# A gated unit in plain float32, in pairs of half-width matmuls, in place of three products of split parts

## The chip, the cores and the metric

The kernel runs on one core of a Trainium2 chip. The metric is the device time of one execution in microseconds. TensorE is called PE in the profile, VectorE DVE, ScalarE ACT, GpSimd POOL and SyncE SP; `PEld` is the load of a stationary operand into TensorE. Line numbers such as L699 are those of the kernel before.

## What is computed

The input is `x` of 2048 tokens by 448 features. It is normalised over the features, and two branches work on the result; their sum and `x` itself are the output.

```python
xn = _layernorm(x, axis=-1)
return x + _A_ref(xn, ...) + _B_ref(xn, B_w_gate, B_w_up, B_w_down)

# _A_ref: a long convolution along the tokens, one kernel of 2048 taps per feature
K = 2.0 * jnp.einsum("dn,dnl->dl", C, P).real      # P = exp(A dt * position), 256 states
y = irfft(rfft(u, 4096) * rfft(K, 4096))[:2048] + u * D_skip

# _B_ref: the gated unit, 1792 hidden features
g = jnp.einsum("bsd,df->bsf", x, w_gate)
u = jnp.einsum("bsd,df->bsf", x, w_up)
return jnp.einsum("bsf,fd->bsd", _sigmoid(g) * u, w_down)
```

All inputs and outputs are float32.

## The kernel before

Two generators, `conv()` and `glu()`, yield small steps, each with a weight that stands for its length, and a loop at the end always advances the generator that has done the smaller share of its total. So the two branches are spread over each other evenly, and the instruction order on each engine follows from that; `hp(HP)` gives an instruction a high priority, `tc.issue_after(x)` keeps one behind another. The totals stand in a list, where 14.8 is the planned length of one hidden tile of the gated unit:

```python
total = [sum(Y0) + 11 * WP + 8 * WX + 14 + NCK * WK + HOLE + 17 * WS, 2 * (4 + NFT * 14.8) - HELD]
```

`conv()` has three stages.

- A first stage loads and normalises x, transposes it for the gated unit (`x_transpose`), and prepares the parameters of the convolution kernels (`prep`, on DVE and ACT), with a first transform of x (`x_spec`).
- The generator `kgen` makes the convolution kernels in 56 steps of 8 features. In each step, POOL makes tables of magnitudes (`magnitudes`, L495 and L507), TensorE makes phases (`tr`, L529), ACT takes their sines (L537 to L540), DVE multiplies both (`Et` and `Ft`, L591 to L593), and TensorE sums over the states (`ko`, L607, four tiles of 32 columns side by side). Every four steps two banks of small 64x64 products follow (`kp` and `kq`, L555).
- `spectra` goes over frequencies in 17 steps. `there` transforms kernels and x (`sp`, L892), DVE multiplies them, `back` transforms to the time domain (`pv`, L919), a copy goes through memory (`v_d`, `vp`), and `last` makes the last transform (`pv`, L954) and adds it to the accumulators.

All these products but `tr` are of plain float32. In `there`, the output is made in halves of 64 partitions: for each of two feature halves `j` and each of two sources, the two real and imaginary parts `c` and two frequencies `i` make four matmuls, where `i` selects the half of the output partitions. At the single frequency step (`k == 32`, the `sx,t` and `skl,t` groups of the profile) there is one `i`, so all of its matmuls go to one half.

`glu()` takes the tokens in two halves of 1024, each as two blocks `t` of 512, and the hidden features in 14 tiles of 128, in groups of three or two (`FCH`). For each hidden tile and each `t` there is one gate: `gate` makes g and u in two PSUM banks named `gu` (four in all, shared with the down products `po`), ACT takes a tanh (`th`), and DVE makes `hf` from both. After each group the down products add it, for eight blocks of 128 tokens, to accumulators in SBUF (`acc`, L815).

TensorE takes float32r operands here, which have fewer bits than float32. So each operand is split into a high part and the rest: x into `xh` and `xl` (with the last 64 of the 448 features packed as high and low in `xr`), the weights into `wh` and `wl`, the hidden activations into `hh` and `hl` (L715, L717), the down weights into `dh` and `dl` (L779, L780). A product is then three: high by high, low by high, high by low. For one gate these are 11 matmuls of 128x128 by 512 columns for g and 11 for u (L699); one block of a down product takes three matmuls of 448 columns per hidden tile (L810). The weights of nine hidden tiles are split once and both parts stored to memory (`wt_d`, `dt_d`), to be loaded again for the second half of the tokens; those of the other five (`RAW`) are loaded and split a second time, on POOL.

Of the kernel before, what the change touches and what calls it, by code (L numbers as in the profile page):

```python
# [15 lines left out]
ALU = mybir.AluOpType  # L16
# [14 lines left out]
WS = 4.5  # L31
# [4 lines left out]
HELD = 9  # L36
# [4 lines left out]
RB = 2  # L41
# [4 lines left out]
RAW = set(GROUPS[0] + GROUPS[1][1:])  # L46
# [82 lines left out]
def s4d_glu_kernel(ctx, tc, io):  # L129
# [14 lines left out]
    wt_d = dram.tile([2, NFT, 128, 8 * 128], F32, name="wt_d")  # L144

    v_d = dram.tile([2, 128, 32, H], F32, name="v_d")
    dt_d = dram.tile([2, NFT, 128, D], F32, name="dt_d")
# [43 lines left out]
    def x_transpose(src, xs, o0):  # L191

        xh, xl, xr = xs
# [6 lines left out]
        for k in range(4):  # L200
            kp = 128 if k < 3 else 64
            at = k * nb % 4
            if nb == 4:
                ps = banks[k]
            elif at == 0:
                ps = psg.tile([128, 512], F32, name="gu", bufs=4)
            for b in range(nb):
                c = 128 * (at + b)
                nc.tensor.transpose(ps[:kp, c : c + 128], src[b][:, 128 * k : 128 * k + kp], ident)
            p = ps[:kp, 128 * at : 128 * (at + nb)]  # L210
            if k == 0 and nb == 2:
                continue
            if k == 1 and nb == 2:
                p = ps.rearrange("p (k t) -> p k t", k=2)
                nc.scalar.copy(xh[:, 0:2, o], p)
                v.tensor_tensor(xl[:, 0:2, o], p, xh[:, 0:2, o], ALU.subtract)
            elif k < 3:
                nc.scalar.copy(xh[:, k, o], p)  # L218
                v.tensor_tensor(xl[:, k, o], p, xh[:, k, o], ALU.subtract)
            else:  # L220
                mv = nc.scalar.copy(xr[0:64, o], p)
                xls[:] = [v.tensor_tensor(xr[64:128, o], p, xr[0:64, o], ALU.subtract)]
                act[:] = [mv]
# [403 lines left out]
    def w_load(f, raw=None, eng=nc.sync):  # L627
        fs = slice(128 * f, 128 * f + 128)
        if raw is None:
            raw = pg.tile([128, 2, 4, 128], F32, name="wraw", bufs=1)  # L630
        for i, nm in enumerate(("B_w_gate", "B_w_up")):
            w = io[nm]
            eng.dma_start(raw[:, i, 0:3], w[0:384, fs].rearrange("(k p) f -> p k f", p=128))
            for h in range(2):
                eng.dma_start(raw[64 * h : 64 * h + 64, i, 3], w[384:448, fs])
        return raw

    def rd_load(f, rd=None, eng=nc.sync):
        if rd is None:
            rd = pg.tile([128, D], F32, name="rd", bufs=RB)  # L640
        eng.dma_start(rd, io["B_w_down"][128 * f : 128 * f + 128])
        return rd

    def w_low():
        return pg.tile([128, 2, 4, 128], F32R, name="wl", bufs=2)

    def d_low():
        return pg.tile([128, D], F32R, name="dl", bufs=FCH[0] + 1)

    def kept(t, d, f):  # L650
        for i in range(2):
            flat = t[i].rearrange("p i k f -> p (i k f)") if len(t[i].shape) == 4 else t[i]
            yield flat.bitcast(F32), d[i, f]

    def pair_load(b):

        xns = [pg.tile([128, D], F32, name="xt", tag=t, bufs=2 * FCH[0]) for t in ("hh", "hl")]
# [16 lines left out]
    def pair_first(b, xns):  # L674

        x1 = pg.tile([128, 2, D], F32, name="x1", tag="wraw", bufs=1)
# [3 lines left out]
        for g in range(4):  # L680
            to = x1[:, g] if g < 2 else pg.tile([128, D], F32, name="x1", tag="rd", bufs=RB)
# [4 lines left out]
    def gate(w, xs, to, between=None):  # L686
        wh, wl = w
        xh, xl, xr = xs
        pgu = []
        for i in range(2):  # L690
            ps = psg.tile([128, 512], F32, name="gu", bufs=4)
            mm = [(wh[:, i, k], xh[:, k]) for k in range(3)]
            mm += [(wh[:, i, 3], xr)]
            mm += [(wl[:, i, k], xh[:, k]) for k in range(3)]
            mm += [(wl[:, i, 3], xr)]
            mm += [(wh[:, i, k], xl[:, k]) for k in range(3)]
            with tc.issue_after(sp_mm[0].ins) if glu_on else nullcontext():
                for n, (a_, b_) in enumerate(mm):
                    glu_mm[:] = [nc.tensor.matmul(ps, a_, b_, start=(n == 0), stop=(n == len(mm) - 1))]  # L699
            pgu.append(ps)  # L700
            if i == 0:
                yield 2.5
# [5 lines left out]
        hf = pg.tile([128, 512], F32, name="hf", bufs=1)  # L708
# [3 lines left out]
        hh = pg.tile([128, 512], F32R, name="hh", bufs=2 * FCH[0])  # L712
        hl = pg.tile([128, 512], F32R, name="hl", bufs=2 * FCH[0])
        with hp(HP):
            nc.scalar.copy(hh, hf)  # L715
        with hp(HP):
            v.tensor_tensor(hl, hf, hh, ALU.subtract)  # L717
        to.append((hh, hl))

    def glu():  # L720
        stores = []
        for half in range(2):
# [4 lines left out]
            for fs_ in ORDER[half]:  # L727
# [14 lines left out]
                for n_, (f, t) in enumerate(order):  # L742
                    if t == 0:
                        wh = pg.tile([128, 2, 4, 128], F32R, name="wh", bufs=2)
                        if half == 0:
                            first = len(raws) == 2
                            raw, rd = raws.pop()
                            wl = w_low()
                            with hp(HP):
                                nc.scalar.copy(wh, raw)  # L750
                                if first:
                                    v.scalar_tensor_tensor(wl, raw, lim[:, 0, 0:1], wh, ALU.mult, ALU.subtract)
                                else:
                                    v.tensor_tensor(wl, raw, wh, ALU.subtract)  # L754
                            if not raws and f + 1 < NFT:
                                raws.append((w_load(f + 1), None))
                            if f not in RAW:
                                stores.extend(kept((wh, wl), wt_d, f))
                        elif f in RAW:
                            raw, wl = w_load(f, eng=nc.gpsimd), w_low()  # L760
                            nc.gpsimd.tensor_copy(wh, raw)
                            nc.gpsimd.tensor_tensor(wl, raw, wh, ALU.subtract)
                        else:
                            wl = w_low()
                            for t_, d_ in kept((wh, wl), wt_d, f):
                                nc.sync.dma_start(t_, d_)
                        ws.append((wh, wl))
                    between = (lambda s_=mid[n_]: step(*s_)) if cross and mid[n_] else None
                    yield from gate(ws[f - f0], xq[2 * half + t], hs[t], between)
                    for t_, d_ in stores:  # L770
                        nc.sync.dma_start(d_, t_)
                    stores.clear()
                    if t == 0:
                        dh = pg.tile([128, D], F32R, name="dh", bufs=FCH[0])
                        if half == 0:
                            rd = rd or rd_load(f)
                            dl = d_low()
                            with hp(HP), tc.issue_after((act if f == 1 else marks)[0].ins):
                                nc.scalar.copy(dh, rd)  # L779
                            nc.gpsimd.tensor_tensor(dl, rd, dh, ALU.subtract)  # L780
                            if f not in RAW:
                                stores.extend(kept((dh, dl), dt_d, f))
                        elif f in RAW:
                            dl = d_low()
                            rd = rd_load(f, pg.tile([128, D], F32, name="rdw", tag="wraw", bufs=1), nc.gpsimd)
                            nc.gpsimd.tensor_copy(dh, rd)
                            nc.gpsimd.tensor_tensor(dl, rd, dh, ALU.subtract)
                        else:
                            dl = d_low()
                            for t_, d_ in kept((dh, dl), dt_d, f):  # L790
                                nc.sync.dma_start(t_, d_)
                        wts.append((dh, dl))
                    yield 2.5
# [4 lines left out]
                for t in range(2):  # L798
                    acc = accs[2 * half + t]
                    for b in range(4):  # L800
# [4 lines left out]
                        bs = slice(128 * b, 128 * b + 128)  # L805
                        n = 0
                        with tc.issue_after(sp_mm[0].ins) if glu_on else nullcontext():
                            for (hh, hl), (dh, dl) in zip(hs[t], wts):
                                for a_, w_ in ((hh, dh), (hh, dl), (hl, dh)):
                                    glu_mm[:] = [nc.tensor.matmul(  # L810
                                        po, a_[:, bs], w_, start=(n == 0), stop=(n == 3 * fc - 1)
                                    )]
                                    n += 1
# [4 lines left out]
                        yield 0.6 * fc  # L818
# [13 lines left out]
    def spectra(pf):  # L832
# [5 lines left out]
        t32 = pg.tile([128, 3, 128], F32, name="t32", tag="rd", bufs=RB)  # L838
# [307 lines left out]
```

## Time and profile before

| | |
|---|---|
| median of three runs | 737.32 us (734.25 to 742.52) |
| the profiled execution | 732.29 us, of which the profile's span is 730.4 |
| mean granted TensorE clock | 0.977 |
| instructions | 19084 |
| moved by DMA | 116.76 MB |

The profile is one execution. Its span runs from the first instruction to the last. Busy times are per engine; matmuls overlap each other, and their recorded ends are modelled, so the rate of a stretch of matmuls is read from their starts. A row such as `L699 PE MATMUL gu<-xh,wh 128*128 128x512 f32 x336 | 101.8, 410` names the line, engine, output and inputs, the tile of the array (rows by columns), the output's shape, the count, the busy time in us and the mean of one in ns. In rows of the chain in order of time, the first number is the start in us, the second the length of the stretch.

### The profile page before, as it was taken

The page shows a single profiled execution, that of the slowest core. Times are in us where ns is not written, and L with a number is a line of the kernel's source. Part 1 is how long each engine was busy: PE and PEld are TensorE (multiplying, and loading weights), DVE is VectorE, ACT ScalarE, POOL GpSimd, SP SyncE. Part 2 cuts the span into 40 slices and gives each one's busy share as a digit, 9 for nine tenths or more (in the row PEclk, how much of TensorE's full clock was granted, in tenths as well). Part 3 has the DMA queues.
Part 4 walks back from the last instruction along what each step waited for, and adds up shares of the span by engine and source line. Part 5 has one row for each costly group of instructions (what it writes and reads, how often), then busy time and mean ns, then how long its engine had stood idle before and what let it go on. Part 6 is the DMA issues. An engine that isn't in the chain of part 4 may idle for free.

```text
span 730.4 us, 19084 instructions
## 1 busy us (share of the span) xinstructions
PE 679.1 (93%) x7780; PEld 534.4 (73%) x7780; DVE 560.4 (77%) x776; ACT 421.1 (58%) x650; POOL 379.7 (52%) x423
## 2 busy tenths in 40 slices
PE   2998799997999999888999999999999999999994
PEld 1765688785887787555878887888877787776783
DVE  5799996798899999889579969977855555564553
ACT  3646364677688787888567778776742222323310
POOL 2120036798788987974655875876844002351001
PEclk9998999997999999999999999999999999999998
DMA  9946338326313562635863242232269999999746
GB/s 209 227 107 201 79 104 273 128 95 197 125 51 110 184 201 68 189 114 178 224 172 123 76 144 84 83 110 68 78 164 271 248 245 243 251 242 249 182 135 162
DMA packets 93288, 116.76 MB, mean 160 GB/s; under 512 B 12177, under 2 KB 81169, under 8 KB 92945
## 3 DMA queue, kind: packets, MB, share of 16 engines
q1 hardware_dynamic: 83888, 95.08, 47.9%
q10 hardware_dynamic: 6736, 14.57, 6.5%
q0 software_dynamic: 2576, 5.90, 3.5%
q8 instruction: 61, 1.00, 0.6%
q14 instruction: 27, 0.21, 0.1%
HBM read 70.75 MB, written 44.76 MB: 158 GB/s over the span
## 4 chain that ended last, share of the span: by engine, by line
PE 60%; DVE 10%; POOL 8%; DMA 8%; ACT 7%; issue 4%; SPq 2%; ACTq 1%; POOLq 0%; DVEq 0%
PE gu L699 23%; PE po L810 15%; PE sp L892 7%; PE ko L607 5%; PE pv L919 4%; PE tr L529 3%; POOL me L507 3%; POOL mf L507 2%; DMA wraw<-in_B_w_up_dram 1%; DVE wl L754 1%; POOL dl L780 1%; PE kp L555 1%; DMA acc<-in_A_u_dram 1%; DMA v_d<-vt 1%; DVE Et L591 1%
## 5 line engine op out<-in xcount | busy, mean ns | idle before, releaser
L507 POOL TENSOR_TENSOR me<-me,pm 128x32 f32<-128x32 f32 (+1 forms) x168 | 141.4, 841 | 89.6 <-DVE Et L592 77.6
L507 POOL TENSOR_TENSOR mf<-mf,pm 128x64 f32<-128x64 f32 (+1 forms) x112 | 127.1, 1135 | 4.7
L699 PE MATMUL gu<-xh,wh 128*128 128x512 f32 x336 | 101.8, 410 | 1.4 <-ACT xh L218 1.4
L699 PE MATMUL gu<-xh,wl 128*128 128x512 f32 x336 | 96.0, 393 | 0.0
L699 PE MATMUL gu<-xl,wh 128*128 128x512 f32 x336 | 95.8, 390 | 0.0
L591 DVE TENSOR_TENSOR Et<-me,S 128x1024 f32<-128x1024 f32 x56 | 82.6, 1475 | 10.1 <-ACT S L540 7.2
L810 PE MATMUL po<-dh,hh 128*128 128x448 f32 x224 | 86.0, 384 | 3.4 <-DVE acc L815 2.5
L810 PE MATMUL po<-dl,hh 128*128 128x448 f32 x224 | 84.3, 376 | 1.1 <-POOL dl L780 1.1
L592 DVE TENSOR_TENSOR Et<-me,S 128x1024 f32<-128x1024 f32 x56 | 77.0, 1375 | 10.1 <-ACT me L520 9.9
L593 DVE TENSOR_TENSOR Ft<-mf,S 128x1024 f32<-128x1024 f32 x56 | 78.3, 1398 | 7.0 <-POOL mf L507 3.1
L810 PE MATMUL po<-dh,hl 128*128 128x448 f32 x224 | 83.0, 373 | 0.0
L537 ACT ACTIVATE S<-tr 128x1024 f32<-128x1024 f32 x56 | 57.8, 1032 | 41.5 <-PE tr L529 39.5
L715 ACT CAST hh<-hf 128x512 fp32r<-128x512 f32 x56 | 34.9, 623 | 76.8 <-DVE hf L710 60.8
L699 PEld LDWEIGHTS gu<-xh,wh 128*128 128x128 f32 x336 | 62.4, 193 | 19.8 <-issue 3.4
L699 PEld LDWEIGHTS gu<-xh,wl 128*128 128x128 f32 x336 | 63.5, 189 | 15.1 <-DVE pl L306 0.7
L607 PEld LDWEIGHTS ko<-Et,Ft 128*32 128x32 f32 x3584 | 54.4, 111 | 26.7 <-issue 13.0
L699 PEld LDWEIGHTS gu<-xl,wh 128*128 128x128 f32 x336 | 63.0, 188 | 14.0 <-issue 0.7
L607 PE MATMUL ko<-Et,Ft 128*32 128x64 f32 x3584 | 64.5, 222 | 8.1 <-DVE Ft L593 6.3
L540 ACT ACTIVATE S<-S,hpi 128x1024 f32<-128x1024 f32 x56 | 65.5, 1170 | 2.9 <-DMA acc<-in_A_u_dram 2.9
L815 DVE SCALAR_TENSOR_TENSOR acc<-po,acc 128x448 f32<-128x448 f32 x80 | 48.5, 617 | 22.6 <-PE po L810 22.5
L717 DVE TENSOR_TENSOR hl<-hf,hh 128x512 fp32r<-128x512 f32 x56 | 49.6, 886 | 19.6 <-ACT hh L715 19.6
L710 DVE SCALAR_TENSOR_TENSOR hf<-th,gu 128x512 f32<-128x512 f32 x56 | 38.1, 681 | 31.1 <-PE gu L699 25.9
(196 smaller groups left out, 1284.2 us busy)
## 6 DMA issues: line engine op xcount, KB each, us to landing
sk_d<-sk ACTq DMA_DIRECT2D x14, 512.0 KB
sx<-x_d SPq DMA_DIRECT2D x32, 224.0 KB
skl<-sk_d SPq DMA_DIRECT2D x16, 448.0 KB
vp<-v_d SPq DMA_DIRECT2D x16, 448.0 KB
v_d<-vt SPq DMA_DIRECT2D x62, 112.0 KB
wt_d<-wh SPq DMA_DIRECT2D x9, 512.0 KB
wt_d<-wl SPq DMA_DIRECT2D x9, 512.0 KB
wl<-wt_d SPq DMA_DIRECT2D x9, 512.0 KB
```

What stands on the lines that cost most here:

```text
L507: ins = nc.gpsimd.tensor_tensor(m[:, :, w + a : 2 * w : n], m[:, :, a:w:n], par(base + i).unsqueeze(2).to_broadcast([128, 4 * DC, w // n]) ...
L537: nc.scalar.activation(rows(cs), pv, AF.Abs)
L540: sins[:] = [nc.scalar.activation(cs, cs, AF.Sin, scale=-TWO_PI, bias=hpi)]
L591: v.tensor_tensor(Et[:, :, :, 32:64], two(me[:, :, 32:64]), S[:, 1::-1], ALU.mult)
L592: v.tensor_tensor(Et[:, :, :, 0:32], two(me[:, :, 0:32]), S[:, 1:3, :, ::-1], ALU.mult)
L593: fts[:] = [v.tensor_tensor(Ft, two(mf), S[:, 3:5], ALU.mult)]
L607: nc.tensor.matmul(ko[32 * j : 32 * j + 32, sl], Ft[:, cc, DC * h + 4 * q + j], Et[:, cc, DC * h + 4 * q + j], start=(k == 0), stop=(k == ...
L699: glu_mm[:] = [nc.tensor.matmul(ps, a_, b_, start=(n == 0), stop=(n == len(mm) - 1))]
L717: v.tensor_tensor(hl, hf, hh, ALU.subtract)
L810: glu_mm[:] = [nc.tensor.matmul(po, a_[:, bs], w_, start=(n == 0), stop=(n == 3 * fc - 1))]
L815: v.scalar_tensor_tensor(acc[:, b], po, 0.5, acc[:, b], ALU.mult, ALU.add)
L892: mm = nc.tensor.matmul(to, tb[:kk, t, 64 * c : 64 * c + 64], rhs, start=True, stop=True, skip_group_check=True,)
```

## The change

The gated unit works on float32 as it is. x is kept as one tile `xs` (three blocks of 128 features, and the last 64 in both partition halves of a fourth), the weights `w` and `wd` are used as loaded, the activations as `hf`. Nothing is split, stored or loaded split. Each product of 128 output columns is made as two matmuls of 64 output columns, one after the other. For the last 64 features of a gate, the products of g take the upper 64 rows and those of u the lower 64, both at the end of the gate. Each hidden tile's weights are loaded for both halves of the tokens, on SP's queue, two tiles ahead (`weights`, `queue`, `loaded`). The planner's weights of the gated unit's steps change with it, and so does the interleaving.

```diff
-HELD = 9
+HELD = 5.7
+WG = 1.3
+WR = 0.45
+WD = 0.38
...
-        xh = pg.tile([128, 3, 512], F32R, name="xh", bufs=2)
-        xl = pg.tile([128, 3, 512], F32R, name="xl", bufs=2)
-        xr = pg.tile([128, 512], F32R, name="xr", bufs=2)
-        return xh, xl, xr
+        return pg.tile([128, 4, 512], F32, name="xs", bufs=2)
...
+    def weights():
+        if queue:
+            f = queue.pop(0)
+            loaded.append((w_load(f), d_load(f)))
...
     def gate(w, xs, to, between=None):
-        wh, wl = w
-        xh, xl, xr = xs
         pgu = []
+
+        def part(i, k, rows, start=False, stop=False):
+            for c in range(2):
+                cs = slice(64 * c, 64 * c + 64)
+                glu_mm[:] = [nc.tensor.matmul(
+                    pgu[i][cs], w[rows, i, k, cs], xs[rows, k], start=start, stop=stop,
+                    skip_group_check=True,
+                )]
+
         for i in range(2):
-            ps = psg.tile([128, 512], F32, name="gu", bufs=4)
-            mm = [(wh[:, i, k], xh[:, k]) for k in range(3)]
-            mm += [(wh[:, i, 3], xr)]
-            mm += [(wl[:, i, k], xh[:, k]) for k in range(3)]
-            mm += [(wl[:, i, 3], xr)]
-            mm += [(wh[:, i, k], xl[:, k]) for k in range(3)]
+            pgu.append(psg.tile([128, 512], F32, name="gu", bufs=4))
             with tc.issue_after(sp_mm[0].ins) if glu_on else nullcontext():
-                for n, (a_, b_) in enumerate(mm):
-                    glu_mm[:] = [nc.tensor.matmul(ps, a_, b_, start=(n == 0), stop=(n == len(mm) - 1))]
-            pgu.append(ps)
+                for k in range(3):
+                    part(i, k, slice(0, 128), start=(k == 0))
+                if i == 1:
+                    for r in range(2):
+                        part(r, 3, slice(64 * r, 64 * r + 64), stop=True)
...
-        hf = pg.tile([128, 512], F32, name="hf", bufs=1)
+        hf = pg.tile([128, 512], F32, name="hf", bufs=2 * FCH[0] + 1)
...
-        with hp(HP):
-            nc.scalar.copy(hh, hf)
-        with hp(HP):
-            v.tensor_tensor(hl, hf, hh, ALU.subtract)
-        to.append((hh, hl))
+        to.append(hf)
...
                         with tc.issue_after(sp_mm[0].ins) if glu_on else nullcontext():
-                            for (hh, hl), (dh, dl) in zip(hs[t], wts):
-                                for a_, w_ in ((hh, dh), (hh, dl), (hl, dh)):
+                            for n, (hf, d) in enumerate(zip(hs[t], wts)):
+                                for c in range(2):
+                                    ts = slice(128 * b + 64 * c, 128 * b + 64 * c + 64)
                                     glu_mm[:] = [nc.tensor.matmul(
-                                        po, a_[:, bs], w_, start=(n == 0), stop=(n == 3 * fc - 1)
+                                        po[64 * c : 64 * c + 64], hf[:, ts], d,
+                                        start=(n == 0), stop=(n == fc - 1), skip_group_check=True,
                                     )]
...
-    total = [... , 2 * (4 + NFT * 14.8) - HELD]
+    total = [... , 2 * (4 + NFT * (4 * WG + 2 * WR + 8 * WD)) - HELD]
```

More of the change, by code (lines that the diff above doesn't have):

```diff
@@ L743, in glu @@
                     if t == 0:
[L744 to L766, printed above, removed]
@@ L767, in glu @@
[L767 removed]
+                        w, d = loaded.pop(0)
+                        weights()
+                        ws.append(w)
+                        wts.append(d)
                     between = (lambda s_=mid[n_]: step(*s_)) if cross and mid[n_] else None
                     yield from gate(ws[f - f0], xq[2 * half + t], hs[t], between)
[L770 to L772 removed]
@@ L773, in glu @@
[L773 to L792, printed above, removed]
```

82 lines of the change are left out of this document (27 added, 55 removed).

## The prediction

> **What bounds the kernel now.** I read the page's busy shares first, then the shares by engine of the chain that ended last, and then a table of the five stages (before the first `ko` product of the kernel generator; the generator; a gap; the spectra; the tail).
>
> ```profile
> PE 679.1 (93%) x7780; PEld 534.4 (73%) x7780; DVE 560.4 (77%) x776; ACT 421.1 (58%) x650; POOL 379.7 (52%) x423
> ...
> PE 60%; DVE 10%; POOL 8%; DMA 8%; ACT 7%; issue 4%; SPq 2%; ACTq 1%; POOLq 0%; DVEq 0%
> ```
> ```profile
> core 0: us, PE busy (x) PEld busy (x) DVE busy (x) ACT busy (x) POOL busy (x), PEclk, DMA share, GB/s
> 0.00:143.00 143.00, 120.12 (x557) 93.52 (x557) 117.08 (x227) 75.49 (x122) 41.56 (x59) 0.96 0.65 169
> 143.00:542.00 399.00, 381.79 (x5752) 305.16 (x5751) 344.59 (x362) 298.35 (x439) 299.52 (x318) 0.98 0.42 128
> 542.00:549.00 7.00, 6.51 (x88) 5.27 (x90) 2.60 (x2) 2.16 (x4) 4.42 (x5) 1.00 0.40 129
> 549.00:710.00 161.00, 160.12 (x1232) 122.04 (x1230) 89.33 (x176) 45.07 (x86) 29.89 (x37) 1.00 0.95 230
> 710.00:730.40 20.40, 10.59 (x160) 8.44 (x158) 6.84 (x12) 0.00 (x0) 4.34 (x8) 0.83 0.64 170
> ```
> TensorE is idle for 51 us of 730.4: 23 before the generator, 17 in it, 1 in the spectra, 10 in the tail. Everywhere else it is issuing, so a microsecond of TensorE issue added or taken is nearly a microsecond of time. A busy TensorE isn't one at its peak; what counts is how often a matmul starts. DVE stands second (345 of 399 in the generator), and DMA is near full in the spectra (0.95).
>
> **What a matmul costs.** The chain in order of time has long runs of one kind, whose starts give the rate.
>
> ```profile
> 522.39 3.85 PE po L810 x18
> 526.24 2.51 PE gu L699 x11
> ...
> 530.44 2.49 PE gu L699 x11
> ...
> 601.87 1.71 PE pv L919 x16
> 603.58 3.18 PE sp L892 x32
> ...
> 624.91 2.72 PE gu L699 x11
> ```
> Eleven full-width products of 512 columns take 2.50 us (0.227 each); a down product of 448 columns takes 0.21 (3.85 over 18). Those inputs are float32r. No plain-float32 matmul of 512 columns stands in the trace, so I price it from the plain-float32 ones of the spectra, which are also pairs of 64-column halves:
>
> ```profile
> L892 PE MATMUL sp<-skl,tb 128*64 128x224 f32 x256 | 30.5, 359 | 0.3 <-ACT vt L925 0.3
> L892 PE MATMUL sp<-sx,tb 128*64 128x224 f32 x256 | 29.6, 352 | 0.0
> L699 PE MATMUL gu<-xh,wl 128*128 128x512 f32 x336 | 96.0, 393 | 0.0
> ```
> ```profile
> 559.71 0.92 PE L892 MATMUL sp<-sx,t 64*64 64x224 f32 x4
> 560.47 0.92 PE L892 MATMUL sp<-skl,t 64*64 64x224 f32 x4
> ...
> 566.50 0.98 PE L892 MATMUL sp<-skl,tb 128*64 128x224 f32 x8
> 567.31 0.93 PE L892 MATMUL sp<-sx,tb 128*64 128x224 f32 x8
> 568.06 0.93 PE L892 MATMUL sp<-skl,tb 128*64 128x224 f32 x8
> 568.82 0.93 PE L892 MATMUL sp<-sx,tb 128*64 128x224 f32 x8
> ```
> Here the count decides. The program calls L892 eight times per source in each of 16 full steps (two `j`, two `c`, two `i`), 128 in all, and the trace holds 256. So each plain-float32 call becomes two matmuls, while a float32r call stays one (six `xh,wl` calls in each of 56 gates make 336). From 567.31 to 568.82 run sixteen records, eight calls, four pairs: 0.3775 us per pair of 224 columns, or 1.685 ns per column. A lone half is no cheaper than a pair: the `sx,t` step, whose halves all lie in one column half, takes 0.76 us for four records, two calls, so 0.38 per call. The two halves of a pair thus do run at the same time, and the pair costs two matmuls of two clocks per column each.
>
> Scaled by columns, a pair of 512 costs 0.863 us and one of 448 costs 0.755. The 64-row remainder is four tiles of 64x64. The trace has this form in the small products `kp`/`kq`:
>
> ```profile
> 231.21 0.22 PE L555 MATMUL kp<-wk,ks 64*64 64x64 f32 x1
> 231.22 0.22 PE L555 MATMUL kq<-wk,ks 64*64 64x64 f32 x1
> 231.23 0.22 PE L555 MATMUL kp<-wk,ks 64*64 64x64 f32 x1
> 231.23 0.22 PE L555 MATMUL kq<-wk,ks 64*64 64x64 f32 x1
> 231.27 0.22 PE L555 MATMUL kp<-wk,ks 64*64 64x64 f32 x1
> ```
> Four start within 0.02 us and the next four 0.06 later, which is what one such record of 64 columns takes alone (0.19 x 64/224 = 0.054). So all four run together and the remainder costs 0.863 per gate; if only column neighbours overlapped, it would be 1.73.
>
> **The change part by part.**
> Gates, 56 of them. Removed: 22 products, 5.00 us. Added: six pairs, 5.18, and the remainder, 0.86, together 6.04. 56 x 1.04 = +58.
>
> Down products, 224 blocks of 128 tokens by one hidden tile. Removed: three at 0.21, or 0.62 in the long run of 45 quoted below. Added: one pair, 0.755. 224 x 0.135 = +30.
>
> ```profile
> 706.98 9.31 PE po L810 x45
> ```
> Changes of tile shape. Entering another shape costs time: the first eight `sp` records after `pv` take 0.81 us (566.50 to 567.31) and the later eight 0.755; the `pv` run takes 1.71 for sixteen records that would need 1.51 at the rate of `sp`; eleven gate products after `sp` take 2.72 and not 2.50. So a change costs 0.1 to 0.22; I take 0.15. Each gate gets two (into the 64-row tiles and out): 56 x 0.3 = +17, bounds +11 and +25. The phase products `tr` stay full-width, so leaving them is now a change: 54 x 0.15 = +8. From `sp` to a gate there is none any more: about 14 x 0.22 = -3. Together +22.
>
> Splitting work on other engines. Removed are hi/lo copies and subtractions:
>
> ```profile
> L717 DVE TENSOR_TENSOR hl<-hf,hh 128x512 fp32r<-128x512 f32 x56 | 49.6, 886 | 19.6 <-ACT hh L715 19.6
> L715 ACT CAST hh<-hf 128x512 fp32r<-128x512 f32 x56 | 34.9, 623 | 76.8 <-DVE hf L710 60.8 <-DMA out_dram<-ac 10.0 <-issue 5.9
> L780 POOL TENSOR_TENSOR dl<-rd,dh 128x448 fp32r<-128x448 f32 x14 | 24.1, 1718 | 39.5 <-ACT dh L779 39.5
> ```
> with the weights' casts and subtractions, some 75 us of DVE, 55 of ACT and 50 of POOL. None of these engines is the bound, so this pays only where TensorE stood waiting.
>
> ```profile
> PE tr L209 <- DVE xn L267: 12.4, 1, 12.4
> ```
> Of its idle time 12.4 us come before the first matmul (the loads and the norm of x, which stay; the row is from the waits) and 10 in the tail (output stores, which stay). Of the other 29, and of some slow-clock stretches beside them (0.96 and 0.98 in the first two rows above), bounds are 0 and 35 gained; I take 17, about the generator's idle time, because DVE there falls from 86% to some 70% busy and the products come out later relative to it.
>
> Weights. The stores and reloads of split weights (`wt_d`, `dt_d`) go; each of the 28 tile loads is now raw, on SP's queue, two tiles ahead. A tile lasts two gates and eight blocks, 18 us, so a load has some 36 us; I cost this at nothing. If that cover failed, a wait of one load would stand in each of 28 tiles, and SP's other issues behind it. The second half's weight preparation on POOL goes too. DMA in the spectra only gets lighter.
>
> `gate` now ends both accumulators at its end, so `th` comes after all of it and not after its first half:
>
> ```profile
> L707 ACT ACTIVATE th<-gu 128x512 f32<-128x512 f32 x56 | 33.7, 603 | 37.1 <-PE gu L699 37.1
> L710 DVE SCALAR_TENSOR_TENSOR hf<-th,gu 128x512 f32<-128x512 f32 x56 | 38.1, 681 | 31.1 <-PE gu L699 25.9 <-ACT th L707 4.9
> ```
> The four `gu` buffers hold two gates, and 6 us of the next gate cover the 1.3 us of `th` and `hf`. Cost nothing; uncovered, 1.3 us at the end of each of ten groups, 13.
>
> Sum: 730.4 + 58 + 30 + 22 - 17 = 823 span, and 1.9 around it (732.29 against 730.4), 825. The three timed runs lie 0.3 to 1.4% above the profiled one; I add 0.4% and forecast **828**. By stage, with the counts of the changed instruction list (12 gates and 42 blocks, 33 and 134, 11 and 48): about 151 to the first `ko`, 470 for the generator, 205 for the rest.
>
> **Rivals.**
> *Plain float32 at half rate, as the new planner weights suppose* (WG 1.3, WR 0.45, WD 0.38): a pair of 448 then costs 0.38 and a gate 3.05. TensorE would lose 56 x 1.95 + 224 x 0.24 = 163 us, and other engines would set the time: about 130 for the first stage (DVE), 325 for the generator (DVE's 345 less its share of splitting, plus gaps), 170 to 190 for the rest (DMA): **about 640**. It decides if one call is one matmul. For it speak only those weights; against it the doubled count. 4%.
> The Trainium skill's Perfetto Trace Analysis, section Engine Utilization, says that TensorE's output rate is halved for FP32_LOW_HIGH. The trace agrees for one record (0.19 us for 224 columns against 0.10 scaled from float32r), but two records stand for each call, which that rule doesn't say; taken per call it gives this rival's time.
>
> *The remainder's four tiles don't overlap by rows*: +0.86 x 56 = 48, **875**. The gates issue column neighbours first, `kp`/`kq` row neighbours; otherwise the form is the same. 7%.
>
> *Pairs don't overlap at 512 columns*: gates and blocks nearly double, 56 x 5.2 + 224 x 0.75 = +460, **about 1290**. The `sp` pairs speak against it. 2%.
>
> *More waits go than I think*, and changes of shape cost the lower bound: 825 - 18 - 8, **about 800**; same mechanism, inside the range.
>
> **How the numbers follow.** My forecast, with its waits and changes of shape anywhere between the bounds, has 87%. The range runs from 800 (35 us of waits gone, changes at 0.1) to 866, which reaches towards the serial remainder. Faster by over 1% (what a measurement of this kernel can tell from no change) needs the half rate: 4%. Within 1%: 1%. Slower: 95%.
>
> **What would show it.** Right: two records per gate and down call (1344 of 128*64 and 448 of 64*64 at the gate's line, 896 at the down line); eight 512-column records (two pairs) run in about 1.73 us; TensorE idle below 45 us; DVE near 485 us busy; the last `ko` near 620. Wrong: one record per call, or an engine other than TensorE that runs without a gap in the generator.

## The result, and the profile after

The changed kernel takes 834.27 us (829.99 to 835.17, four runs) against 736.91 us of the kernel before on the same chip: 1.130 times as long, 95% interval 1.122 to 1.138. The forecast was 828 (800 to 866). The profiled execution took 835.17 us, its span is 833.4. Of the twelve runs of one variant below (downs alone, at full width) four took 744 to 746 us at a granted clock of 0.977 to 0.979, and its time is that of the other eight.

The page's busy shares and the shares by engine of the chain that ended last, of the changed kernel:

```profile
PE 797.7 (96%) x8564; PEld 339.8 (41%) x8564; DVE 468.3 (56%) x698; ACT 371.8 (45%) x560; POOL 234.7 (28%) x354
...
PE 84%; DVE 7%; DMA 4%; SPq 2%; issue 1%; ACT 1%; POOL 0%; POOLq 0%; DVEq 0%
```

TensorE is now 84% of the chain, where it was 60%. It stands idle for 35.7 us, where it was 51. DVE lost 92 us of work and GpSimd 145, and it helped little: neither set the time. (The prediction had some 75 and 50. On GpSimd more went than the splitting: its tables of magnitudes got shorter too, `mf` of 128x64 from 916 to 408 ns a record. Why, no run isolates, and the profile's spans there are rough.)

The table of the five stages, of the changed kernel (its first `ko` product is at 156.2 us, its last at 620.2; the third stage is the gap up to the first `sp`):

```profile
core 0: us, PE busy (x) PEld busy (x) DVE busy (x) ACT busy (x) POOL busy (x), PEclk, DMA share, GB/s
0.00:156.20 156.20, 137.16 (x668) 44.09 (x668) 95.85 (x200) 55.90 (x91) 30.71 (x62) 0.97 0.59 147
156.20:620.20 464.00, 461.07 (x6250) 191.04 (x6250) 285.26 (x319) 273.79 (x388) 197.98 (x282) 1.00 0.24 69
620.20:636.40 16.20, 11.54 (x135) 4.30 (x124) 1.38 (x2) 2.93 (x5) 0.54 (x1) 0.96 0.65 168
636.40:806.00 169.60, 169.46 (x1320) 91.78 (x1322) 77.77 (x163) 38.22 (x74) 1.13 (x2) 0.98 0.81 203
806.00:833.40 27.40, 18.43 (x210) 8.58 (x206) 8.08 (x14) 0.97 (x2) 4.38 (x8) 0.87 0.57 151
```

Stage by stage the span grew by 13 us (143.0 to 156.2), by 65 (399 to 464), and by 25 in the last three together (188.4 to 213.2). In the generator TensorE is idle for 2.9 us (464.00 less 461.07), where it was 17.2.

The groups of the changed lines, kept apart by form, of the changed kernel:

```profile
L673 PE MATMUL gu<-xs,w 128*64 128x512 f32 x1344 | 324.1, 604 | 4.2 <-DVE hf L695 4.2
L744 PE MATMUL po<-wd,hf 128*64 128x448 f32 x896 | 186.1, 552 | 3.3 <-DVE acc L749 2.4 <-DVE xs L212 0.9
...
L673 PE MATMUL gu<-xs,w 64*64 64x512 f32 x448 | 64.2, 615 | 0.0
```

The counts are two records for each call. The busy time of such a row is no cost, since two halves overlap (1344 records of 604 ns would be 812 us). The cost is in the chain in order of time, where a stretch shows what a whole gate (32 records) or a run of down pieces (four records each) takes:

```profile
565.29 6.32 PE gu L673 x32
...
642.43 6.17 PE gu L673 x32
...
661.09 6.32 PE gu L673 x32
...
680.79 4.51 PE po L744 x24
...
808.78 11.45 PE po L744 x60
```

The first gate takes 6.32 us behind a full-width product (`tr`), the second 6.17 behind one of halves (`sp`). The 32 records of the third row also stand behind `sp`, but by their starts they are u's bank, the remainder and the next gate's first bank: with the remainder in the middle it is 6.32 again. A down piece takes 0.752 us (4.51 over six) to 0.763 (11.45 over fifteen).

Two of TensorE's waits are new. The waits of TensorE, of the changed kernel (us in total, times, longest):

```profile
PE tr L202 <- DVE xn L256: 12.2, 1, 12.2
PE sp L826 <- DMA skl<-sk_d: 4.7, 1, 4.7
PE gu L673 <- DVE hf L695: 4.2, 1, 4.2
```

The first was there before. For the second, the chain in order of time shows what the load `skl` stood behind:

```profile
620.75 3.81 PE gu L673 x20
...
624.58 0.38 SPq L621
...
628.72 0.61 SPq L796
...
630.70 5.62 DMA skl<-sk_d
...
636.46 5.97 PE sp L826 x32
```

and the waits of SP's queue from 600 to 640 us, with its issues as the timeline gives them for the kernel before:

```profile
SPq L621 <- PE gu L673: 16.9, 1, 16.9
```
```profile
525.41 0.62 SPq L862 DMA_DIRECT2D sx<-x_d  x1
...
530.47 0.39 SPq L867 DMA_DIRECT2D skl<-sk_d  x1
```

L621 loads gate weights `w`. It waited 16.9 us until the gate that held the buffer was done (620.75 + 3.81 = 624.56), and the first loads of the spectra (L796 and what follows) stood behind it on SP's queue. Before, they were issued at 525 to 531, some 18 us ahead of the first `sp` at 549; now the last is issued at 630.70, and `sp` waits for it.

The third wait has its own chain, in the first stage:

```profile
27.09 9.27 DMA xe<-in_A_u_dram
...
37.02 1.66 DVE st L234 x3
...
38.90 0.58 DVE hf L695
...
39.52 8.09 PE gu L673 x28
```

The `hf` that frees `gu` stood on DVE behind statistics of x (`st`), which waited for a load. So this wait comes from what lies ahead of `hf` on DVE, not from a late `th`.

### The profile page after: what moved, and what is told of

It is laid out like the page before. It is cut to its first block, busy times and chain, and to the rows that moved or that the text cites. A ratio compares the mean times of both kernels' runs of the same rounds, so it can differ in the third digit from the quotient of the medians.

```text
span 833.4 us, 20328 instructions
## 1 busy us (share of the span) xinstructions
PE 797.7 (96%) x8564; PEld 339.8 (41%) x8564; DVE 468.3 (56%) x698; ACT 371.8 (45%) x560; POOL 234.7 (28%) x354
## 4 chain that ended last, share of the span: by engine, by line
PE 84%; DVE 7%; DMA 4%; SPq 2%; issue 1%; ACT 1%; POOL 0%; POOLq 0%; DVEq 0%
PE gu L673 39%; PE po L744 20%; PE sp L826 7%; PE ko L596 7%; PE tr L518 4%; PE pv L853 3%; DMA xe<-in_A_u_dram 1%; PE kp L544 1%; DMA aim<-in_A_A_imag_dram 1%; DVE pl L303 1%; DMA w<-in_B_w_gate_dram 1%; DVE m L303 1%; PE gu L267 1%; DMA skl<-sk_d 1%; DVE pl L297 1%
## 5 line engine op out<-in xcount | busy, mean ns | idle before, releaser
L673 PE MATMUL gu<-xs,w 128*64 128x512 f32 (+1 forms) x1792 | 383.3, 606 | 4.2 <-DVE hf L695 4.2
L673 PEld LDWEIGHTS gu<-xs,w 128*64 128x64 f32 (+1 forms) x1792 | 105.0, 136 | 231.4 <-issue 213.1
L744 PE MATMUL po<-wd,hf 128*64 128x448 f32 x896 | 186.1, 552 | 3.3 <-DVE acc L749 2.4
L496 POOL TENSOR_TENSOR me<-me,pm 128x32 f32<-128x32 f32 (+1 forms) x168 | 117.2, 698 | 249.9 <-DVE Et L581 227.5
L744 PEld LDWEIGHTS po<-wd,hf 128*64 128x64 f32 x896 | 62.9, 138 | 104.3 <-issue 93.5
L692 ACT ACTIVATE th<-gu 128x512 f32<-128x512 f32 x56 | 33.6, 600 | 145.7 <-PE gu L673 134.5
L526 ACT ACTIVATE S<-tr 128x1024 f32<-128x1024 f32 x56 | 57.5, 1026 | 85.0 <-PE tr L518 84.7
L496 POOL TENSOR_TENSOR mf<-mf,pm 128x64 f32<-128x64 f32 (+1 forms) x112 | 88.4, 790 | 5.7
L527 ACT ACTIVATE S<-tr 128x1024 f32<-128x1024 f32 x56 | 57.4, 1025 | 0.0
L518 PE MATMUL tr<-sel,ph 128*128 128x512 f32 x112 | 41.2, 448 | 0.0
L826 PE MATMUL sp<-skl,tb 128*64 128x224 f32 x256 | 32.1, 373 | 4.7 <-DMA skl<-sk_d 4.7
```

The source lines that it names most:

```text
L496: ins = nc.gpsimd.tensor_tensor(m[:, :, w + a : 2 * w : n], m[:, :, a:w:n], par(base + i).unsqueeze(2).to_broadcast([128, 4 * DC, w // n]) ...
L518: nc.tensor.matmul(ps[:, h], ph[:, cn % 2, 128 * h : 128 * h + 128], sel, start=True, stop=True)
L526: nc.scalar.activation(rows(cs), pv, AF.Abs)
L527: nc.scalar.activation(rows(S[:, 0:5:4]), pv, AF.Sin, scale=TWO_PI)
L673: glu_mm[:] = [nc.tensor.matmul(pgu[i][cs], w[rows, i, k, cs], xs[rows, k], start=start, stop=stop, skip_group_check=True,)]
L744: glu_mm[:] = [nc.tensor.matmul(po[64 * c : 64 * c + 64], hf[:, ts], d, start=(n == 0), stop=(n == fc - 1), skip_group_check=True,)]
```

## The experiments

The times of the kernel before in these comparisons are 735 to 739 us; the ratios are to those.

**The remainder alone.** Changed kernel without the last 64 features:

```diff
-                    part(i, k, slice(0, 128), start=(k == 0))
-                if i == 1:
-                    for r in range(2):
-                        part(r, 3, slice(64 * r, 64 * r + 64), stop=True)
+                    part(i, k, slice(0, 128), start=(k == 0), stop=(k == 2))
```

> Leaves out the products of the last 64 features of every gate, and changes nothing else of the changed kernel (834 us). Theory (TensorE's issue sets the time, and entering another tile shape costs issue time too): per gate 0.86 us of four tiles and two changes of shape of 0.13 each go, 56 x 1.12 = 63, so 771 us. Rival (changes of shape are free): 56 x 0.86 = 48, so 786. Rival (another engine already sets the time): over 800.

770.53 us (ratio 1.046, 1.041 to 1.052). The remainder costs 63.7 us, 1.14 per gate: 0.86 if its four tiles cost what a pair costs, and 0.28 for changes of shape and whatever else came with it. The chain in order of time, of this run:

```profile
590.51 5.15 PE gu L673 x24
```

Six pairs take 5.15 us behind `sp`, 0.858 each. With the remainder at the end of the same stretch it was 6.17, and with the remainder between two banks 6.32. Less 0.86 that leaves 0.16 for one change of shape more, and 0.31 for two. So a change costs some 0.16 us of issue time. Four 64x64 tiles do run at once: in halves of two they would need another 0.86, and there is no room for it.

**One more pair per gate.**

```diff
-                for k in range(3):
+                for k in (0, 1, 2, 2)[: 4 - i]:
```

> Makes one pair of each gate twice (features 256 to 383 of g are added once more), so seven pairs and the remainder. Theory: one pair of 512 columns costs 0.859 us and all of it shows, 56 x 0.859 = +48, so 882 us. Rival (TensorE is only busy on paper and another engine or the DMA sets the time): under 850.

873.42 us (1.185, 1.179 to 1.191), 39 more than the changed kernel. In the chain of this run the gate itself grew by the full price, 7.18 - 6.32 = 0.86:

```profile
598.62 7.18 PE gu L673 x36
```

So 48 us of issue came to 39 of time. TensorE's idle time is 4.7 us less than in the changed kernel (31.0 against 35.7), which is half of the difference. TensorE's issue is the bound, but not to the last microsecond.

**Full width instead of halves.** One call of 128 columns in place of each pair, in gates and downs:

```diff
-            for c in range(2):
-                cs = slice(64 * c, 64 * c + 64)
-                glu_mm[:] = [nc.tensor.matmul(
-                    pgu[i][cs], w[rows, i, k, cs], xs[rows, k], start=start, stop=stop,
...
+            glu_mm[:] = [nc.tensor.matmul(
+                pgu[i], w[rows, i, k], xs[rows, k], start=start, stop=stop,
...
```

> Plain float32 at full width: one matmul of 128 output columns in place of each pair of 64 (128*128, and 64*128 for the remainder). Theory A (a plain float32 call is two matmuls of two clocks per column whatever its width): 0.86 us per 512 columns as for a pair, so about 834 us, within 15. Theory B (two clocks per column hold for half tiles alone, a full tile needs four): gates +5.2 us each and blocks +0.75, so about 1290 us.

830.85 us (1.126, 1.119 to 1.133), the same within the spread of the runs. Its groups, by form, have half the records:

```profile
L671 PE MATMUL gu<-xs,w 128*128 128x512 f32 x672 | 310.1, 603 | 2.9 <-DVE xs L209 2.9
...
L671 PE MATMUL gu<-xs,w 64*128 64x512 f32 x224 | 81.1, 641 | 0.0
```

A full-width call in plain float32 also takes two records. The pair of halves buys nothing over it. That the times are the same hides two differences. Summed from the start of each record to the start of the next, waits left out, the downs take 172 us at full width and 182 in halves, and the gates 396 and 390: at full width, in 16 of the 56 gates, other work stands between the two parts of the remainder, which then don't run beside each other.

**The halves apart.** Three products for the left half of a bank, then three for the right, and likewise in the downs:

```diff
-                for k in range(3):
-                    part(i, k, slice(0, 128), start=(k == 0))
+                for c in range(2):
+                    for k in range(3):
+                        part(i, k, slice(0, 128), start=(k == 0), halves=(c,))
```

> Same matmuls, but the halves of a pair don't stand side by side: for each bank all products of columns 0 to 63 come first and then those of columns 64 to 127 (and the same in the down products). Theory A (two halves overlap only as neighbours in the order): of six calls only the two in the middle overlap, so a bank's three pairs take 4.3 to 5.2 us and not 2.6, a down block of three 3.0 to 3.8 and not 2.26, which makes +260 to +410, so 1090 to 1240 us. Theory B (TensorE looks far enough ahead to find the other half): 834.

925.16 us (1.256, 1.250 to 1.262): +91, between both theories. The chain of this run:

```profile
622.92 3.63 PE gu L673 x12
...
642.49 7.23 PE gu L673 x32
...
757.25 5.31 PE po L745 x24
```

A bank of twelve records takes 3.63 us alone. Paired it takes 2.57 (half of 5.15 above), one after the other 5.15. So TensorE still ran some of the right half beside the left: 3.63 is what eight steps of 0.43 and some 0.2 for entering come to, four pairs and four records alone. The starts of the twelve records show it. Two stand alone, then four times two start within 0.06 us of each other, then two stand alone. The records don't name their half, but two at a time must be one of each, so the first of the right half, seventh in the program, starts beside the third and ahead of three of the left half that are still to come. A gate costs 0.91 more (7.23 against 6.32), 51 us in all, and more where other work stands between its two banks; a down piece 0.13 more (5.31 against 4.51 over six), some 30. Summed from start to start over the run, the gates take 77 us more and the downs 21, and TensorE waits 8 less. By what rule TensorE chooses what to run beside what, no run here settles.

**Downs alone.** The kernel before, with plain float32 pairs in the downs only. The activations and the down weights are no longer split, and the down weights are loaded as they are for both halves of the tokens:

```diff
-                            for (hh, hl), (dh, dl) in zip(hs[t], wts):
-                                for a_, w_ in ((hh, dh), (hh, dl), (hl, dh)):
+                            for n, (hf, d) in enumerate(zip(hs[t], wts)):
+                                for c in range(2):
...
```

> The kernel before (737 us) with only its down products in plain float32 pairs; the gates keep their 22 products of split parts. Theory: 224 blocks x (0.752 - 0.62) = +30, and some 10 to 15 for changes of shape between gates and down products and from the phase products, less some 10 of waits on the splitting of hf that go: 765 us, 755 to 780. Rival (down products in plain float32 aren't slower, the gates make all of the loss): 737 or less.

744.85 us (1.012, 1.006 to 1.017), only 8 more than before; a miss by 20.

**Gates alone.** The changed kernel with the downs as three products again, the activations split on ACT and DVE, the down weights split on ACT and GpSimd in both halves:

```diff
-        to.append(hf)
...
+        with hp(HP):
+            nc.scalar.copy(hh, hf)
+        with hp(HP):
+            v.tensor_tensor(hl, hf, hh, ALU.subtract)
+        to.append((hh, hl))
...
+                        with hp(HP), tc.issue_after(marks[0].ins):
+                            nc.scalar.copy(dh, d)
+                        nc.gpsimd.tensor_tensor(dl, d, dh, ALU.subtract)
```

> The changed kernel with its down products as before, three products of split parts (hf split on ACT and DVE, the down weights split anew for each half of the tokens on ACT and GpSimd). Theory: 834 less 224 x (0.752 - 0.62) = 30, with some 5 to 10 back for waits on the splitting and changes of shape: 810 us, 800 to 820. Then gates and down products add up. Rival (the loss is in the down products): 760 or less.

807.15 us (1.096, 1.091 to 1.101), as expected. So the parts don't add up: downs first +8, gates after them +89; gates first +70, downs after them +27. Whichever comes first is some 19 us cheaper. The generator's row of the stage tables, first of the run with downs alone, then with gates alone:

```profile
134.80:549.50 414.70, 410.75 (x5910) 269.75 (x5912) 310.21 (x330) 279.88 (x399) 252.92 (x302) 1.00 0.33 107
```
```profile
155.20:597.60 442.40, 437.44 (x6112) 229.56 (x6111) 322.71 (x353) 297.01 (x437) 256.03 (x301) 0.99 0.26 76
```

TensorE is idle there for 4.0 and 5.0 us, against 17.2 before and 2.9 with both. Each part alone fills most of that idle time, so it can be had only once: 13.2 and 12.2 us apart, 14.3 together, which is 11 of the 19 us. The granted clock goes the same way: its mean over the profiled execution is 0.977 before, 0.996 with downs alone, 0.983 with gates alone and 0.983 with both. The span times what is missing to 1 is 17, 3, 14 and 14 us, so downs alone get back 14 of it, gates alone 3, and both together 3. That is an upper estimate of what the clock adds, since some of it falls where TensorE has nothing to do.

**Half the gated unit's work**, to see what the rival of half rate would have given; the downs leave out one hidden tile of each group:

```diff
-                for k in range(3):
-                    part(i, k, slice(0, 128), start=(k == 0))
...
+                for k in range(2 - i):
+                    part(i, k, slice(0, 128), start=(k == 0), stop=(k == 1 - i))
...
+                            for n, (hf, d) in list(enumerate(zip(hs[t], wts)))[: fc - 1]:
```

> Leaves out half of the gated unit's products: three pairs per gate and no remainder, and in the down products one hidden tile less per group. TensorE's work on the gated unit falls from 505 to about 254 us, which is what plain float32 at half rate would make. It prices the first rival of the prediction. If TensorE alone set the time to the end: 834 less 250 less 15 for changes of shape, 570 us. Theory: other engines take over (DVE in the first stage and the generator, DMA in the spectra) and it ends near 640, 615 to 665.

670.81 us (0.910, 0.906 to 0.915). Its page, its waits of TensorE, its clock and the generator's row of its stage table:

```profile
PE 553.9 (83%) x7124; PEld 278.5 (42%) x7124; DVE 483.9 (73%) x698; ACT 368.8 (55%) x560; POOL 308.8 (46%) x354
```
```profile
PE ko L596 <- DVE Ft L582: 18.3, 17, 2.2
PE tr L518 <- ACT S L528: 17.6, 20, 3.1
```
```profile
core 0: 665.7 us, clock 0.926
```
```profile
128.20:480.30 352.10, 305.24 (x5304) 156.13 (x5304) 302.05 (x314) 268.28 (x383) 275.94 (x291) 0.90 0.29 85
```

TensorE now waits for the generator's DVE and ACT, in pieces of up to 3 us, and its granted clock is 0.926 and not 0.983. The rival's 640 was 30 us too low.

**The second half's weight loads on GpSimd's queue.**

```diff
-            loaded.append((w_load(f), d_load(f)))
+            eng = nc.sync if len(queue) >= NFT else nc.gpsimd
+            loaded.append((w_load(f, eng), d_load(f, eng)))
```

> The changed kernel with the weight loads of the second half of the tokens on GpSimd's queue and not on SP's. Theory (at the entry into the spectra a weight load that waits for a buffer holds back, on SP's queue, the first loads of the spectra, so that the first product there waits 5.2 us for skl): that wait goes, 829 us against 834, and the gap between the last ko and the first sp shrinks from 16.2 to some 11 us. Rival (the DMA engines themselves are late, not the queue): the wait stays, 834. Rival (the slower issue on GpSimd delays magnitudes): over 836.

827.72 us (1.123, 1.120 to 1.127), 6.5 less than the changed kernel, as expected. The gap row of its stage table:

```profile
620.40:631.90 11.50, 11.50 (x139) 4.34 (x127) 0.69 (x1) 2.33 (x4) 4.18 (x7) 1.00 0.36 110
```

It lasts 11.5 us instead of 16.2, TensorE has no idle time in it, and the wait for `skl` is gone. The queue was the cause. The Trainium skill's DMA: Bandwidth & Descriptors, section Issuing engines are not separate DMA queues, says that starting DMAs from several engines saves only the sequencer's time to start them, which is usually small. Here it saved 6.5 us, because an issue that waits for a buffer holds up all issues behind it; the measurement decides.

**Downs alone, at full width.** The same as downs alone, but one call per piece:

```diff
+                            for n, (hf, d) in enumerate(zip(hs[t], wts)):
+                                glu_mm[:] = [nc.tensor.matmul(
+                                    po, hf[:, bs], d, start=(n == 0), stop=(n == fc - 1)
+                                )]
```

> The kernel before with its down products in plain float32 at full width (one matmul of 128 columns in place of the pair), gates as before. Against the pairs (745 us): theory, changes of shape cost issue time, and at full width there is none between gates, down products and phase products, so some 20 + 18 changes of 0.13 go, -5: 740 us. Rival (changes of shape cost nothing that shows): 745.

734.8 us (ratio 0.998, 0.994 to 1.002): no difference from before, and 10 us under the pairs, where 5 were expected. The full width has no change of shape to and from the float32r gates, which is the likely reason: summed from start to start, the downs take 170 us here and 184 in pairs. Three float32r products or one plain product of full width: for the downs both give the same time here, though a piece alone costs 0.13 us more.

**Mixed, and the end split.** Two attempts to take the better of both. The first has plain downs at full width in the first half of the tokens only, and the second half as three products with the weights split on GpSimd. The second has plain downs everywhere but in the last two groups of the second half, which are three products split on GpSimd:

```diff
+                    yield from gate(ws[f - f0], xq[2 * half + t], hs[t], between, half == 0)
...
-                        yield 0.6 * fc
+                        yield (0.6 if half else 0.75) * fc
```
```diff
+                plain = half == 0 or fs_ not in ORDER[1][-2:]
...
-                        yield 0.6 * fc
+                        yield (0.75 if plain else 0.6) * fc
```

> Down products of the first half of the tokens in plain float32 at full width (that is where DVE is most loaded and TensorE waits), those of the second half as three products, their weights split on GpSimd. Theory: +15 of TensorE's issue for 112 blocks, and some 18 of the waits on the splitting go: 734 us, a little faster than before (737). Rival (the waits of the first half stay, as they come from other work): 752.

> The kernel before with every down product plain at full width, but for the last two groups of the second half, which stay three products of parts with their weights split on GpSimd. Theory (TensorE's issue decides in the spectra, and GpSimd is idle there): against the run with all down products plain at full width (738 us), 48 pieces by about 0.135 us less, some 6.5 us: 731 us (727 to 736), about 1% under the kernel before. Rival (splitting on GpSimd, or what it holds up, brings waits as in the mixed run, 749): 738 us or more.

749.07 us (1.013, 1.009 to 1.017) and 758.34 us (1.030, 1.026 to 1.035). The theory of each fell. The generator's row of the stage table, then the gate records (22 a gate) in the generator and after it, of the run with full-width downs:

```profile
136.90:538.40 401.50, 397.72 (x5632) 279.81 (x5631) 313.53 (x329) 280.81 (x400) 262.59 (x305) 1.00 0.34 109
```
```profile
136.90:538.40 401.50, 177.71 (x730) 1.00 0.34 109
538.40:733.00 194.60, 53.99 (x220) 0.99 0.81 209
```

The same rows of the run with the end split:

```profile
136.40:537.90 401.50, 383.74 (x5541) 270.53 (x5544) 305.82 (x318) 279.31 (x398) 256.58 (x303) 0.96 0.35 110
```
```profile
136.40:537.90 401.50, 169.97 (x675) 0.96 0.35 110
537.90:757.00 219.10, 66.14 (x275) 0.97 0.77 190
```

The generator lasts 401.5 us in both. But in the second, 2.5 gates fewer lie in it (675 records against 730, over 22) and as many more behind it, and TensorE idles there for 17.8 us instead of 3.8, at a granted clock of 0.96 instead of 1.00. What was not done beside the generator is done after it: the rest takes 24 us longer (218.4 against 194.3). The gates are 12 of these (66.14 against 53.99 us busy); the other half isn't accounted for. The mixed run shows the same, with twelve gates behind the generator and not ten. The likely reason is my own edit: both kernels state 0.75 to the planner for a plain piece and the other 0.6, so the planner takes the gated unit to be further on than it is. That was not tried alone. Both kernels also have fewer buffers for activations and down weights than the one with full-width downs, and split weights on GpSimd in the second half; these rivals are not tested either.

**DVE relieved alone.** The kernel before without the subtraction `hl`:

```diff
-            v.tensor_tensor(hl, hf, hh, ALU.subtract)
-        to.append((hh, hl))
+        to.append((hh, hh))
```

> The kernel before without the subtraction that makes hl (50 us of DVE); the third product of each down product uses hh a second time, so TensorE's work is the same. Theory (TensorE stands waiting where DVE is loaded, so plain down products get back some 20 us of waits and cost little): 717 us, 710 to 725. Rival (DVE's load costs nothing, and the small loss of plain down products has another reason): 737.

730.94 us (0.990, 0.985 to 0.994): 7.7 us, a third of what was expected. The generator's row of its stage table:

```profile
140.40:537.20 396.80, 374.90 (x5726) 299.37 (x5725) 316.59 (x327) 297.68 (x437) 286.02 (x315) 0.98 0.40 127
```

DVE has 28 us less to do there, and TensorE is still idle for 21.9 us. So a lighter DVE doesn't remove that idle time.

## Why the prediction was right, and where it was not

**The sum, term by term.** Summed from the start of each record to the start of the next, waits left out, TensorE spends 82 us more on the gates than before (390 against 308), 36 more on the downs (182 against 146) and 4 more on `tr`; its waits between its first and its last product are 15 less. The prediction's terms were 58 + 17 - 3, 30, 8 and 17. So each has the right sign, and the gates and downs are some 10 and 6 us short. The 0.4% that it added for the timed runs did not come, as the profiled execution is the longest of the four; without it the forecast would have been 825.

**The price of a plain-float32 pair: right.** Scaled from the `sp` products it was 0.863 us for 512 columns and 0.755 for 448; measured are 0.858 and 0.752 to 0.763. The whole forecast rests on the count of two records a call and on these starts. Full width at the same time and the pairs torn apart show the same from two sides: what counts is columns times two records, and halving costs little only while the halves stand together.

**The remainder and the changes of shape: right.** 0.863 and 0.30 per gate were forecast, 1.14 together was measured, and a change costs 0.16 where 0.15 was taken. The step had two changes for every gate; where the remainder stands last, the work behind it would have changed shape anyway, and only one is added. The Trainium skill's TensorEngine Tiling (Array Packing), section Key Properties, says that a change of the tiling mode drains TensorE. The trace agrees, at 0.16 us a change, and with 10 us more time for downs in halves than at full width among full-width gates.

**The waits: right in size, wrong in reason.** I took 17 us; TensorE's idle time fell by 15.6, and by 14.3 in the generator. The granted clock there rose from 0.98 to 1.00 besides, worth some 8 us of 399, which the bounds had and the 17 had not. I wrote that DVE falls to 70% there and the products come out later relative to it. The first half of that step failed: with DVE relieved alone, the idle time stays. The second half stands. In five kernels (before, downs at full width, mixed, the end split, DVE relieved) TensorE is busy for 375 to 398 us in the generator, and that stage lasts 397 to 401.5 us; only with more work than that does it grow with TensorE. So the 17 us were room beside the generator that new TensorE work filled at no cost. It is not a fixed floor: with half the gated unit's work the stage took 352 us. And what sets the 400 us, no run isolates.

**The weights' loads, costed at nothing: wrong by 6.5 us.** The step priced the load's own lateness and had "SP's other issues behind it" only as an aside to a load that fails to be covered. The load was in time, and its wait for a buffer still held up the spectra. The stages show it: 205 us were forecast for the rest, 213.2 measured. Some 4 us more lie in the plan: 340 gate records after the last `ko` are 10.6 gates, where it was 10.0. The prediction's count of the new list had 11 gates there, but its 205 is close to what ten gates come to (188.4 + 10 x 1.34 + 48 x 0.135 - 3). These are the rows, first of the changed kernel (32 records a gate), then of the one before (22 a gate):

```profile
620.20:636.40 16.20, 10.20 (x52) 0.96 0.65 168
636.40:834.00 197.60, 58.02 (x288) 0.97 0.78 195
```
```profile
542.00:549.00 7.00, 5.30 (x22) 1.00 0.40 129
549.00:731.00 182.00, 48.34 (x198) 0.98 0.91 222
```

**The end of a gate, costed at nothing: no cost seen.** TensorE waited for `hf` once, 4.2 us, in the first stage, and that came from DVE's order. This stage ended at 156.2 and not at 151; what else made it longer is open. The generator took 464 where 470 was forecast, so the errors partly cancel: that the total is only 0.8% over the forecast is in part luck. The three stages of the prediction add up to 826, not to the 823 of its sum; the span came out 0.9% above the one and 1.3% above the other (833.4).

**The rivals.** The serial remainder falls by the run without it. Pairs that don't overlap fall by the six pairs in 5.15 us of the same run. The half rate falls by the count of records. By the run with half the work it would have given some 671 us and not 640: I had left out the short waits between DVE, ACT and TensorE, and the lower clock that was granted beside them.

## What to carry over

Read the price of a matmul from starts in a stretch of the same kind, and count records per call: plain float32, with two records of 0.43 us each for 512 columns, was not cheaper here than three products of a type with one record of 0.23, however many split operations on other engines went with it. Idle time of the bound engine beside a long stage is room that can be filled once, so edits that fill it don't add up, and a plan that moves work out of that stage pays for the work in full. A DMA issue that waits for a buffer held up everything behind it on its queue, so put a prefetch that waits on another queue than loads with a deadline.

## What was not expected of the hardware

Plain float32 costs the same at full width as in two halves (830.85 and 834.27 us). TensorE starts records of one half ahead of up to three of the other that stand before them in the program: with the halves of a bank apart, the seventh record starts beside the third, and twelve take 3.63 us, between 2.57 and 5.15. With half the gated unit's work the granted clock was 0.926, against 0.983.
